# Cosine attention and a highway layer in one kernel: work shared out anew over the engines, and a new order

## The chip, the cores and the metric

The kernel runs on one core of one Trainium2 chip. The metric is device time in microseconds. A core has five instruction streams: PE (TensorE, products and transposes; its weight loads are shown as PEld), DVE (VectorE), ACT (ScalarE), POOL (GpSimd) and SP (SyncE, which here only issues transfers). Each works through its own instructions strictly in order and waits on semaphores for the others. ACT and POOL issue transfers too.

## The reference, cut to what matters

```python
# q, k, v: (8, 12, 448, 64) = batch, head, position, channel; float32
q_n = q / (norm(q, axis=-1) + 1e-06)
k_n = k / (norm(k, axis=-1) + 1e-06)
attn = softmax(q_n @ k_n.T / tau)            # tau = 0.1
x = (attn @ v) -> (8 * 448, 768)             # heads side by side
H = maximum(x @ w_h, 0)                      # w_h, w_t: (768, 768)
T = 1 / (1 + exp(-(x @ w_t + b_t)))
out = T * H + (1 - T) * x                    # float32
```

## The kernel before

**Tiling.** A batch has 12 heads, taken as three groups (g = 0, 1, 2) of four heads, two "t" by two "s". The 448 positions of a head are seven columns of 64 (NJ = 7). A tile of q or k holds 128 rows, 64 positions of two heads, and for a group 2 x 7 x 64 = 896 elements a row.

**Norms.** For each group of q and of k, `norm` squares the 896 elements (`sq`, line 359 on ACT; four k groups on POOL, line 362) and DVE sums each 64 of them (line 370, `rd2`). From the sums, 1/norm is made for several groups at once. Batch 0 uses a logarithm and an exponential on ACT (`lnexp`, lines 396 and 399). All others use `newton` (lines 381 to 388): a bit trick and two Newton rounds on DVE, seven instructions (`nt`), each of them an entry of its own in the order, so that other DVE work can stand between them. q's squares are scaled by tau, so that its 1/norm carries 1/tau.

**Scaling and turning.** `scale` (line 413) multiplies q and k by 1/norm on POOL into f16 (`qn`, 896 wide, and `kn`, in parts of 512 and 384). `turn` transposes them: early batches on PE (line 425, then a copy from PSUM on DVE, line 433), later ones by transposing transfers from SP (line 428).

**Attention.** PE makes scores (lines 468, 478; for batch 0 line 549), ACT takes their exponential (471, 481, 564), PE multiplies with the values (499, 507; 577, 597), and DVE divides by the row sums (514, 516; 579, 583) into `x`. Values are loaded by POOL in three transfers (lines 315 to 317) and copied into a tile with a column of ones (`vc`, DVE, line 439; the remaining 64 positions by `vt`, POOL, line 449).

**Highway layer.** A unit is 128 rows of `x`, four units a batch, 32 in all, the fourth of each batch half wide. `x` is transposed into `xT` (batch 0 on PE, later by a transfer from SP, line 628). PE multiplies with both weights (lines 659, 662). DVE adds the bias (`za`, 699), ACT takes a tanh (`th`, 713), DVE turns it into the gate 0.5 t + 0.5 (`gt`, 715), forms max(H, 0) - x (`hm`, 710) and multiplies by the gate (`gg`, 735). POOL adds x (`out`, 737), SP stores (744, 747). The last two units are split finer (677 to 732).

**What sets the order.** Nothing is scheduled when the kernel is built. `ORDER` at the top is a written-out list of all entries, 1498 of them; an engine's instructions run in the sequence in which they stand there. `SLOTS` says which buffer of a ring each tile takes, so the order also settles who must free a buffer for whom: the q tile `qr` has two buffers, so batch b's q load waits until POOL has scaled the q of batch b - 2. `HOLD` makes q loads wait for a named instruction. `PORT` names kinds of operation on DVE and POOL: the first such POOL instruction that follows a DVE one in the order waits for that DVE instruction.

**Loads.** q comes by SP as f32, k by POOL as f16 (batch 0's by SP and ACT as f32), the weights by POOL. In the list POOL's first entries are: identity, k of batch 1, the first scalings, three value loads of batch 0, `w_t`, the scalings of groups 1 and 2. `w_h`, k of batch 2 and the other values of batch 1 stand behind the scalings of batch 1's first group.

Of the kernel before, what the change touches and what calls it, by code (L numbers as in the profile page):

```python
# [10 lines left out]
I32 = mybir.dt.int32  # L11
# [9 lines left out]
1 4 24 25 2 6 26 0 242 21 17 27 14 19 29 3 16 18 12 28 9 22 13 5 8 11 40 15 20 42 7 10 43 36 38 41 37 39 52 53 44 68  # L21
65 64 239 45 71 66 46 70 69 32 67 72 256 47 31 50 30 73 54 33 51 114 55 48 88 90 74 112 115 49 246 257 78 75 56 252 77
247 57 248 241 85 240 79 76 91 80 84 113 249 98 96 81 89 86 258 259 60 87 99 260 63 61 82 97 59 58 62 122 261 253 254
92 93 120 94 262 123 95 83 116 121 101 263 117 264 100 280 250 118 138 429 119 106 255 35 276 125 139 124 107 126 102
130 127 103 131 279 104 251 136 128 105 277 245 281 278 129 34 108 109 282 137 430 110 146 111 144 265 175 147 244 266
140 176 141 243 145 132 267 133 268 152 434 134 142 269 179 135 270 177 143 442 192 180 153 193 149 271 178 443 294
438 148 194 286 181 23 196 154 150 283 309 151 195 155 435 197 310 305 198 287 156 306 157 307 158 611 439 160 308 288
275 284 161 159 184 433 285 209 436 289 293 186 210 162 444 290 301 163 299 437 185 302 187 164 300 445 165 440 610
220 166 221 188 182 333 297 967 441 167 334 218 274 219 168 298 446 169 431 273 170 303 447 432 222 171 211 212 304
448 183 213 272 199 449 172 450 321 173 325 451 322 174 214 200 452 317 215 461 326 313 323 316 457 324 312 295 291  # L30
625 315 292 327 460 619 331 296 318 314 311 626 332 201 464 203 328 319 202 320 462 617 475 329 463 345 330 474 458
189 204 459 346 357 190 205 342 338 358 349 335 206 350 347 468 353 618 340 337 348 336 226 467 341 354 227 339 490
343 355 613 344 491 465 789 469 356 466 351 362 455 470 360 352 359 456 620 361 621 615 480 366 363 454 365 481 364
478 367 486 471 368 479 228 229 487 616 385 482 484 483 233 453 234 230 401 485 472 235 476 623 473 492 369 493 477
973 488 504 622 388 489 788 386 624 387 799 505 389 627 231 495 499 628 216 506 629 502 614 390 496 503 494 790 497
630 498 631 370 507 232 612 236 371 217 207 391 500 510 501 508 511 372 373 392 509 632 237 393 374 395 795 633 538
800 512 650 514 539 396 394 515 377 397 638 513 379 516 223 797 528 536 974 519 523 640 529 639 517 518 796 378 537
647 380 417 635 530 641 381 526 531 520 521 644 238 522 527 409 524 398 411 793 525 532 224 534 966 410 535 651 794
642 412 533 643 542 645 399 540 801 798 666 668 541 667 546 413 544 652 545 669 547 543 418 653 548 803 549 660 656
977 419 661 804 550 404 375 402 802 646 403 657 191 405 971 637 664 406 662 566 814 423 663 1142 424 420 978 658 665  # L40
598 791 553 551 659 425 636 654 805 792 400 634 421 648 655 981 552 969 649 554 225 975 806 675 555 680 716 681 677
673 807 692 422 982 674 693 671 569 426 717 567 808 809 676 376 407 686 382 682 672 683 810 670 568 678 811 687 679
570 816 560 979 571 688 684 558 689 427 559 685 561 822 428 708 562 704 574 705 582 575 383 813 709 690 408 706 972
823 576 691 577 818 414 707 696 699 208 578 700 415 698 1156 714 976 710 817 701 572 604 819 697 980 599 715 830 600
711 605 983 984 601 968 820 556 606 694 824 695 821 1152 585 985 712 828 986 846 702 713 573 586 703 583 847 722 724
557 831 1141 987 1148 842 840 988 563 721 825 725 843 989 584 812 720 587 719 841 718 1317 723 602 838 726 834 1002
727 839 592 590 815 835 1153 728 844 564 836 845 593 579 826 829 837 591 994 827 832 588 594 870 760 853 871 852 833
850 996 858 1149 862 995 860 859 851 997 855 848 861 849 580 854 998 729 856 863 589 738 857 736 1150 1006 565 739
1157 1146 737 1007 744 868 740 1154 890 1001 731 732 1147 891 1004 730 1003 869 595 866 763 733 867 581 761 999 1151
864 894 888 865 764 1155 762 895 970 1000 873 878 765 889 876 877 1005 1021 1158 884 603 886 1022 879 875 874 885 776  # L50
872 747 880 991 887 745 607 993 881 748 1008 734 882 1144 892 1159 883 746 990 1145 384 752 749 893 1143 753 735 1009
608 1045 1160 1010 903 1161 899 1162 897 900 1046 992 898 902 596 896 1323 901 1015 904 1069 905 1016 754 755 1070 768
954 756 1017 1019 1018 1324 770 906 771 1020 769 741 766 922 1013 742 772 1037 777 1014 782 1163 1164 1316 1038 1011
1169 743 783 1012 1033 784 1035 778 416 767 1036 1176 1026 773 1030 1029 779 1034 1028 938 1027 1181 1039 1041 1061
# [792 lines left out]
```

## Time and profile before

| | |
|---|---|
| time, median of 3 runs | 282.19 us (281.32 to 286.61) |
| profiled execution | 279.05 us, its span 277.2 us |
| mean granted clock | 0.946 |
| HBM read, written | 39.12 MB, 11.01 MB |

The page of the profile gives the busy time of each engine as a share of the span, and the span in 40 slices of 6.93 us with the clock that PE was granted in tenths. The chain of work is followed back from the last instruction to what released it. A group's row reads: line, engine, operation, tiles, shapes, count, then busy us, mean ns of one, and idle time before it with what ended it. A waits row reads: who waited, for whom, total us, times, longest. Where an instruction row ends in square brackets, that is the engine's idle time just before it and what ended it.

### The profile page before, as it was taken

What the parts mean: (1) busy time and instruction counts of PE and PEld (TensorE: products, weight loads), DVE (VectorE), ACT (ScalarE), POOL (GpSimd) and SP (SyncE); (2) the same over time, 40 slices, a digit from 0 to 9 for tenths busy, and PEclk for the clock granted to TensorE, in tenths of its full rate; (3) what the DMA queues carried; (4) which work ended last, traced back from release to release, by engine and by line L of the source; (5) the groups of instructions that cost most, each with busy time, mean ns of one, the idle gap of its engine ahead of it and who ended that gap; (6) DMA issues with size and microseconds to landing.
All of it is one profiled execution on the core that took longest, in us unless ns stands there. A gap on an engine that the chain in (4) does not pass through costs nothing.

```text
span 277.2 us, 8206 instructions
## 1 busy us (share of the span) xinstructions
PE 238.2 (86%) x3447; PEld 146.5 (53%) x3447; DVE 213.9 (77%) x367; ACT 204.7 (74%) x253; POOL 169.5 (61%) x161
## 2 busy tenths in 40 slices
PE   8256799699989899498896999997999989999990
PEld 3135676365755565255554466564645755575640
DVE  3889669779999988639997678789776766446894
ACT  3396898799998989658788599996889568870230
POOL 2495829939837899138879645789348941330550
PEclk9856599999999999979999899999999999999998
DMA  7999599998599769996889979999879467238565
GB/s 229 290 176 254 161 246 204 216 275 104 60 162 263 115 177 223 135 197 120 125 228 166 201 136 175 194 272 196 113 177 163 82 147 162 66 75 194 139 154 144
DMA packets 77398, 47.93 MB, mean 173 GB/s; under 512 B 53040, under 2 KB 74160, under 8 KB 77360
## 3 DMA queue, kind: packets, MB, share of 16 engines
q1 hardware_dynamic: 54128, 33.57, 53.5%
q0 software_dynamic: 22800, 13.08, 35.1%
q10 hardware_dynamic: 432, 0.75, 0.8%
q8 instruction: 27, 0.44, 0.7%
q14 instruction: 11, 0.09, 0.1%
HBM read 39.12 MB, written 11.01 MB: 181 GB/s over the span
## 4 chain that ended last, share of the span: by engine, by line
PE 43%; DMA 21%; DVE 15%; POOL 10%; issue 6%; ACT 2%; DVEq 0%; POOLq 0%; ACTq 0%
PE banks L662 22%; DMA xT<-x 9%; PE banks L468 6%; PE banks L499 6%; DMA kr<-in_k_dram 6%; PE banks L659 4%; DMA qT<-qn 4%; POOL qn L413 3%; POOL kn L413 3%; DVE tt L715 2%; DVE hm L735 2%; DMA qr<-in_q_dram 2%; ACT E L471 2%; DVE x L516 2%; PE banks L478 1%
## 5 line engine op out<-in xcount | busy, mean ns | idle before, releaser
L471 ACT ACTIVATE E<-banks 128x896 f16<-128x896 f32 x126 | 109.7, 917 | 22.0 <-PE banks L468 20.0
L662 PEld LDWEIGHTS <-xT 128*128 128x128 f16 x576 | 51.9, 99 | 49.9 <-issue 14.1
L737 POOL TENSOR_TENSOR os<-x,hm 128x768 f32<-128x768 f16 (+1 forms) x30 | 44.7, 1493 | 42.9 <-DVE hm L735 20.2
L662 PE MATMUL banks<-wt,xT 128*128 128x384 f16 x288 | 55.3, 333 | 7.0 <-DMA xT<-x 6.9
L662 PE MATMUL banks<-wh,xT 128*128 128x384 f16 x288 | 55.6, 332 | 0.9 <-DVE hm L710 0.9
L370 DVE TENSOR_REDUCE n<-sq 128x14 f32<-128x896 f32 (+1 forms) x50 | 51.1, 1037 | 6.3 <-ACT sq L359 6.3
L413 POOL TENSOR_TENSOR qn<-qr,y 128x896 f16<-128x896 f32 (+1 forms) x24 | 41.0, 1710 | 23.2 <-issue 10.8
L413 POOL TENSOR_TENSOR kn<-kr,y 128x384 f16<-128x384 f16 (+1 forms) x42 | 40.0, 964 | 21.5 <-DVE y L388 7.8
L468 PE MATMUL banks<-qT,kT 64*64 64x448 f16 x504 | 40.0, 365 | 2.8 <-DVE x L516 1.7
L713 ACT ACTIVATE tt<-z 128x768 f16<-128x768 f32 (+1 forms) x32 | 24.2, 764 | 19.8 <-DVE z L699 19.2
L499 PE MATMUL banks<-vp,E 128*128 128x65 f16 x756 | 37.7, 194 | 0.0
L499 PEld LDWEIGHTS <-E 128*128 128x128 f16 x756 | 34.0, 97 | 6.5 <-issue 3.6
L710 DVE SCALAR_TENSOR_TENSOR hm<-banks,x 128x768 f16<-128x768 f32 (+1 forms) x30 | 25.7, 858 | 13.1 <-PE banks L662 10.2
L499 PE MATMUL banks<-vp,Et 128*128 128x65 f16 x252 | 34.3, 192 | 0.0
L699 DVE TENSOR_TENSOR z<-banks,bias 128x768 f32<-128x768 f32 x24 | 22.9, 952 | 9.6 <-PE banks L662 9.4
L359 ACT ACTIVATE sq<-qr 128x896 f32<-128x896 f32 (+1 forms) x24 | 22.1, 935 | 5.3 <-DMA qr<-in_q_dram 3.7
L499 PEld LDWEIGHTS <-Et 128*128 128x128 f16 x252 | 24.9, 99 | 0.0
L715 DVE TENSOR_SCALAR tt<-tt 128x768 f16<-128x768 f16 (+1 forms) x32 | 21.8, 683 | 2.7 <-ACT tt L713 2.7
L516 DVE TENSOR_TENSOR x<-banks,rd 128x896 f16<-128x896 f32 x21 | 22.9, 1089 | 0.5
L481 ACT ACTIVATE Et<-banks 128x896 f16<-128x896 f32 x21 | 19.0, 917 | 4.5 <-PE banks L478 4.4
L468 PEld LDWEIGHTS <-kT 64*64 64x64 f16 x504 | 12.6, 105 | 17.7 <-issue 15.2
L359 ACT ACTIVATE sq<-kr 128x896 f32<-128x896 f16 x17 | 16.1, 951 | 5.1 <-DMA kr<-in_k_dram 4.7
(74 smaller groups left out, 301.4 us busy)
## 6 DMA issues: line engine op xcount, KB each, us to landing
out_dram<-os SPq DMA_DIRECT2D x47, 192.0 KB, 3.3
qr<-in_q_dram SPq DMA_DIRECT2D x6, 1344.0 KB, 7.4
kr<-in_k_dram POOLq DMA_DIRECT2D x7, 672.0 KB, 12.9
vr<-in_v_dram POOLq DMA_DIRECT2D x8, 384.0 KB, 7.7
qr<-in_q_dram SPq DMA_DIRECT2D x6, 448.0 KB, 6.8
vr<-in_v_dram POOLq DMA_DIRECT2D x8, 288.0 KB, 9.4
out_dram<-os SPq DMA_DIRECT2D x15, 96.0 KB, 2.6
wt<-in_moe_w_t_dram POOLq DMA_DIRECT2D x1, 1152.0 KB, 13.8
```

The source lines that it names most:

```text
L359: nc.scalar.activation(dst, src, AF.Square, scale=sc)
L370: nc.vector.reduce_sum(R("n2", b)[:, c : c + 7 * n], a, axis=AX.X)
L413: ENG[eng].tensor_mul(o[:, :, t0:t1, :], a, y.unsqueeze(3).to_broadcast([128, hi - lo, t1 - t0, D]))
L468: nc.tensor.matmul(R("B", ("S", n, c))[64 * x : 64 * x + 64, t, 0:S], lhsT=keys(i, s, t, 2 * c + x), rhs=queries(t, s), start=True, stop=True)
L471: op("ACT", f"exp {n} {c}", lambda c=c, n=n: nc.scalar.activation(R("E", n)[:, 14 * c : 14 * c + 14, :].rearrange("l (t j) x -> l t (j x)" ...
L499: nc.tensor.matmul(U[:, 2 * c + t, :], lhsT=(E if m < NC else Et)[:, at : at + 2, :].rearrange("l j x -> l (j x)"), rhs=vp[:, 3 * t + m if ...
L516: op("DVE", f"ev14 {i}", lambda: nc.vector.tensor_mul(R("x", b)[:, :, 128 * g : 128 * g + 128].rearrange("l j (s d) -> l s j d", s=2), U_( ...
L662: nc.tensor.matmul(R("B", at)[:, mh, 0:MH], lhsT=xT[:, cc, :], rhs=w_[:, cc, MH * mh : MH * mh + MH], start=(cc == 0), stop=(cc == CC - 1))
L710: step("hm", n, lambda n=n, P=P: nc.vector.scalar_tensor_tensor(out=cut(R("hm", g), n), in0=P(n), scalar=0.0, in1=xs(n), op0=ALU.max, op1= ...
L713: op("ACT", f"th{nb} {g}", lambda: nc.scalar.activation(R("tt", g)[:, 0:W], R("z", g)[:, 0:W], AF.Tanh, scale=0.5), r=[("z", g), ("t0",)], ...
L715: op("DVE", f"gt{nb} {g}", lambda: nc.vector.tensor_scalar(out=R("tt", g)[:, 0:W], in0=R("tt", g)[:, 0:W], scalar1=0.5, scalar2=0.5, op0=A ...
L737: op("POOL", f"out{nb} {g}", lambda: nc.gpsimd.tensor_add(view(R("os", g)), xs(None), view(R("hm", g))), r=[("gg", g), xk], w=[("os", g)], ...
```

## The change

- `newton`: the seven steps are one entry of the order, and so stand together on their engine.
- tau leaves q's squares. The exponentials of the scores take `scale=1/tau` instead.
- `MOVED` names entries that run on another engine than their kind does. Gates (`gt`): 14 full and 3 half ones from DVE to POOL, among them the last unit's. Value copies (`vc`): seven full and two half ones from DVE to POOL. `vt`: eleven from POOL to DVE. Squares from ACT: with what was already elsewhere, 14 of 896 elements are now on POOL (four before) and nine of them and three halves on DVE (one half before). q loads: the first group of batch 1 and the whole of batches 4 to 7 are issued by ACT (five instructions).
- `FILL`: 46 products of zeros, of the kind of the 18 that the kernel begins with, into a PSUM buffer that nobody reads. 29 stand ahead of the first transpose, 8 ahead of the first scores, 4 and 5 around the second group's transposes.
- `PORT` loses the product with the gate (`gg`); `HOLD` keeps four entries of nine, for q loads that SP issues.
- A new order of all entries, and new buffers with it. POOL's first entries are now: identity, k of batch 1, the values of batch 0, both weights, k of batch 2, one value load of batch 1, then the first scaling. A square of batch 1 stands ahead of the third group's scaling. ACT takes the norms of group 1 ahead of the squares of batch 1. Batch 7's k load stands 32 entries ahead of the transposing transfer of unit 12 (14 before); batch 6's k load stands 14 entries behind that of unit 9 and 3 ahead of that of unit 10. The q loads of batches 4 to 7 on ACT stand 37, 34, 15 and 49 entries behind the scaling that frees their buffer.

```diff
-HOLD = {239: 44, 240: 57, 241: 252, 429: 121, 610: 56, 788: 57, 966: 53, 1141: 537, 1316: 161}
-
-PORT = ("nt", "gt", "gg", "vc", "qn", "kn", "vt", "out", "cx", "ou")
+HOLD = {240: 50, 241: 113, 417: 115, 592: 292}
+MOVED = {'sq1 q 0 0 0': 'DVE', 'vc3 0 3 0': 'POOL', 'vt 0 0': 'DVE', 'gt6 0': 'POOL', 'ldq 1 0': 'ACT',
...
+PORT = ("nt", "gt", "vc", "qn", "kn", "vt", "out", "cx", "ou")
...
-        o = Op(eng, name, fn, w, r, u, mode)
+        o = Op(MOVED.get(name, eng), name, fn, w, r, u, mode)
...
-    WARM, FILL, NLATE = 18, (), 2
+    WARM, FILL, NLATE = 18, (29, 8, 4, 5), 2
...
-                if eng == "ACT":
-                    nc.scalar.activation(dst, src, AF.Square, scale=sc)
-                elif eng == "POOL":
-                    assert sc == 1.0
-                    nc.gpsimd.tensor_mul(dst, src, src)
+                if on[-1] is nc.scalar:
+                    nc.scalar.activation(dst, src, AF.Square)
                 else:
-                    nc.vector.scalar_tensor_tensor(out=dst, in0=src, scalar=sc * sc, in1=src, op0=ALU.mult, op1=ALU.mult)
+                    on[-1].tensor_mul(dst, src, src)
...
-        def step(j):
+        def steps():
...
-            if j == 0:
-                v_.tensor_scalar(out=y.bitcast(I32), in0=n2.bitcast(I32), scalar1=-0.5,
-                                 scalar2=float(0x5F3759DF), op0=ALU.mult, op1=ALU.add)
-            elif j in (1, 4):
+            v_.tensor_scalar(out=y.bitcast(I32), in0=n2.bitcast(I32), scalar1=-0.5,
+                             scalar2=float(0x5F3759DF), op0=ALU.mult, op1=ALU.add)
+            for _ in range(2):
                 v_.tensor_mul(t, y, y)
...
-        for j in range(7):
-            op("DVE", f"nt{hi - lo} {b} {lo} {j}", lambda j=j: step(j), r=[("n2", b) + p for p in parts] if j == 0 else [("nt", i, j - 1)],
-               w=[("nt", i, j)] + ([("y", b) + p for p in parts] if j == 6 else []), u=[("tu", i), ("n2", b), ("y", b)])
+        op("DVE", f"nt{hi - lo} {b} {lo}", steps, r=[("n2", b) + p for p in parts], w=[("y", b) + p for p in parts],
+           u=[("tu", i), ("n2", b), ("y", b)])
...
-                op("DVE", f"gt{nb} {g}", lambda: nc.vector.tensor_scalar(
+                op("DVE", f"gt{nb} {g}", lambda: on[-1].tensor_scalar(
...
             for o in pl.ordered(ORDER, SLOTS):
                 n = len(nc.cur_bb.bb.instructions)
+                on.append(ENG[o.eng])
                 o.fn()
```

The loads, `scale`, `copy_v`, `copy_vt` and the output sum take their engine from `on[-1]` in the same way, and the exponentials get their scale; the lists `ORDER` and `SLOTS` are replaced.

75 lines of the change are left out of this document (36 added, 39 removed), and 110 rows, old and new, of the table ORDER.

## The prediction

> **What bounds the kernel now.** I read the page's busy times and slices first, then windows, then the chain of work that ended last.
>
> ```profile
> PE 238.2 (86%) x3447; PEld 146.5 (53%) x3447; DVE 213.9 (77%) x367; ACT 204.7 (74%) x253; POOL 169.5 (61%) x161
> PEclk9856599999999999979999899999999999999998
> PE 43%; DMA 21%; DVE 15%; POOL 10%; issue 6%; ACT 2%; DVEq 0%; POOLq 0%; ACTq 0%
> 0.00:20.00 20.00, 10.30 (x95) 5.58 (x95) 13.05 (x26) 10.58 (x18) 10.35 (x17) 0.79 1.03 231
> 20.00:40.00 20.00, 15.72 (x341) 13.00 (x342) 15.60 (x43) 16.69 (x22) 12.16 (x14) 0.70 0.88 221
> 60.00:80.00 20.00, 19.10 (x357) 13.15 (x355) 18.35 (x26) 19.58 (x25) 16.47 (x15) 1.00 0.86 118
> 76.70:200.40 123.70, 109.86 (x1529) 65.00 (x1524) 102.53 (x156) 101.49 (x125) 85.68 (x75) 0.97 1.01 178
> 220.00:240.00 20.00, 19.18 (x268) 11.50 (x266) 12.56 (x20) 13.42 (x18) 8.19 (x5) 1.00 0.69 145
> ```
>
> (A window's columns after its length: PE, PEld, DVE, ACT, POOL busy, each with its count; then clock, DMA share, GB/s.) No engine binds throughout. The first 40 us are a ramp: PE is busy 26.0 of 40, at clocks 0.79 and 0.70. From 60 to 80 us PE, DVE and ACT are all over 18 of 20, so taking work off one of them gives little. In the long middle none is above 89%, PE has 13.8 us of holes there, and POOL has most room (38 us). Late, only PE is full. DMA is a fifth of the chain. So a new order can win the ramp and the holes, not the full stages.
>
> **The ramp.** On the chain's pieces (start, length) and the waits:
>
> ```profile
> 13.24 0.71 POOL vr L317
> 13.95 0.75 POOL vr L316
> 14.70 0.75 POOL vr L315
> 15.44 0.84 POOL wt L321
> ...
> 16.75 1.70 POOL qn L413
> ...
> 34.07 16.36 DMA kr<-in_k_dram
> ```
> ```profile
> POOL qn L413 <- DVE kn L413: 8.4, 1, 8.4
> ```
>
> POOL's first four late loads (0.71 + 0.75 + 0.75 + 0.84 = 3.05 us) stand on the chain ahead of the second head group's scaling. The new order issues those four, both weights, batch 2's k and a third of batch 1's v ahead of the first scaling, in the 8.4 us in which POOL now only waits: 3.05 for the four and about 0.8 for each of three more, 5.5 us, fit. If that cover were gone, each would cost its 0.8 us. At most 3.05 is gained; next late are the second head group's norms, which ACT's new order takes before batch 1's squares. I take −2 (0 to −3.05). The k of batch 2, issued at 34.07 and landing 16.36 us later, leaves POOL some 25 us earlier; it held up ACT, and behind it PE:
>
> ```profile
> 50.51 0.95 ACT L359 ACTIVATE sq<-kr 128x896 f32<-128x896 f16 x1 [2.32 <-DMA kr<-in_k_dram]
> ```
>
> −2 (0 to −2.32); with DMA shares of 1.03 and 0.88 in the ramp the bytes cannot all come sooner, so not more.
>
> **The norm as one unit.** Seven Newton steps, now strung between other DVE work:
>
> ```profile
> 22.95 0.89 DVE L381 TENSOR_SCALAR y<-n 128x28 int32<-128x28 int32 x1
> ...
> 28.64 0.19 DVE L388 SCALAR_TENSOR_TENSOR y<-tu,y 128x28 f32<-128x28 f32 x1
> 29.06 0.84 POOL L413 TENSOR_TENSOR kn<-kr,y 128x384 f16<-128x384 f16 x1 [2.44 <-DVE y L388]
> ```
> ```profile
> POOL kn L413 <- DVE y L388: 7.8, 2, 5.3
> ```
>
> First to last is 5.88 us. At 0.89 for the first and six at about 0.19 they last 2.0 in a row, so the result can come 3.8 sooner; POOL waited 2.44 for it, on the chain, and 5.3 at a later norm, off it. −2 (0 to −2.44). The other side: DVE's queue behind the first step waits 2.0 us instead of pieces of it; that is at most 1 us for a PSUM read, seven times, mostly where DVE has room.
>
> **Products of zeros.** 46 matmuls of 512 columns. The clock is 0.5 to 0.6 in slices 3 to 5, 14 to 35 us, and transposes differ with it:
>
> ```profile
> 1.26 5.81 PE L280 MATMUL banks<-wz 128*128 128x512 f16 x18 [1.26 <-DVE wz L264]
> 12.19 0.93 PE L425 MATMUL banks<-ident,qn 128*128 128x128 f16 x7 [5.12 <-POOL qn L413]
> 46.58 0.56 PE L425 MATMUL banks<-ident,kn 128*128 128x128 f16 x7
> ```
>
> 18 take 5.81 us, 0.32 each, so the first 29 last at most 9.4 us, 5.6 at the ratio 0.56/0.93 of a fast clock, and end between 12.7 and 16.5, where the first transpose now starts at 12.19. The 17 behind (5.5 us at most) lie between transposes and products that wait anyway. Gain: 0.37 us for each of four early transposes, about −1.5; price: an overrun of 0.5 to 4.3 us. I take +0.5 (−1.5 to +4). The Trainium skill ("TensorE: Matmul & The Clock Gate", Part 1: The HAM clock gate) says the clock is halved by default, and opens after one busy window of about 3.4 us; by that the zeros keep it open if no gap is longer, and the term is its lower end (sum −11.5, time 275). The slices' 9, 8, 5 agree with a clock that falls when PE idles.
>
> **Work moved.**
>
> ```profile
> L715 DVE TENSOR_SCALAR tt<-tt 128x768 f16<-128x768 f16 x24 | 18.1, 759 | 2.1 <-ACT tt L713 2.1
> L715 DVE TENSOR_SCALAR tt<-tt x32: 242/354/2476, 57.7 to 270.9; 128x768 f16<-128x768 f16 x24, 128x384 f16<-128x384 f16 x8
> L439 DVE COPY vp<-vr 128x1152 f16<-128x1152 f16 x14 | 9.2, 657 | 0.0
> L449 POOL COPY vp<-vr 64x384 f16<-64x384 f16 x16 | 8.3, 520 | 7.9 <-DVE hm L735 4.6 <-issue 1.3 <-DMA vr<-in_v_dram 0.7
> masks.py:199 POOL TENSOR_SCALAR_AFFINE_SELECT ident<-ident 128x128 f16<-128x128 f16 x1 | 0.3, 292 | 0.1
> L362 POOL TENSOR_TENSOR sq<-kr 128x896 f32<-128x896 f16 x4 | 6.7, 1676 | 3.9 <-DVE n L370 3.8
> L359 ACT ACTIVATE sq<-qr 128x896 f32<-128x896 f32 x23 | 21.5, 951 | 5.3 <-DMA qr<-in_q_dram 3.7 <-DVE n L370 1.6
> L364 DVE SCALAR_TENSOR_TENSOR sq<-qr 128x448 f32<-128x448 f32 x1 | 0.6, 616 | 0.0
> ```
>
> Gates: 14 full and 3 half ones go to POOL. A gate's median on DVE is 0.354 and its worst 2.476: it waits there while POOL works. 14 × 0.759 = 10.6 us leave DVE. On POOL no gate is in the trace. Between a one-input 128-element operation (0.292) and a 384-element copy (0.520) the slope is 0.89 ns an element, which gives 0.86 for 768; the two-input 896-element square, 1.676, is the upper bound. I take 0.86, nearer in kind. The Trainium skill ("GPSIMD Engine Reference", 4.1 Engine selection) speaks against such moves: elementwise work belongs on VectorE, POOL being some twice as slow with two inputs and about line-rate with one. Squares agree (1.676 against ACT's 0.951). If line-rate means 768 elements at that page's 1.2 GHz, a gate would be an estimated 0.64 and POOL's sum 3 us less.
>
> Squares: POOL gains ten (16.8 us), DVE nine of 896 at up to 2 × 0.616 (11) and two halves; ACT loses 19 (18.1) and takes five q issues at 0.50:
>
> ```profile
> 0.74 0.50 ACTq L306 DMA_DIRECT2D E<-in_k_dram  x1
> ```
>
> Value casts: seven full go to POOL (by the slope 1.2 each, 8.4; upper 1.68), 4.6 us leave DVE; eleven 64-row casts (5.7) leave POOL for about 0.2 each on DVE. New sums: ACT 204.7 − 18.1 − 1.1 + 2.5 = 188; DVE 213.9 − 10.6 − 1.4 − 5.5 + 2.2 + 11 + 1.2 = 211; POOL 169.5 + 12.0 + 1.6 + 16.8 + 9.8 − 5.7 = 204. The longest engine stays PE. On the path: of DVE's share in the chain I credit the long gate waits, 17/32 of the four or five that stand there at 1.4 to 1.8: −2.5 (0 to −4). ACT's relief counts only in 60 to 80, where PE has 0.9 left: −0.5. POOL's square of batch 1 ahead of the third group's scaling puts +1.7 into the ramp, half of it covered: +1. The gate on POOL is 0.5 longer and queues; behind it wait only product, sum and store, no PSUM bank: 0, and up to 1 where it ends the tail.
>
> **Queues and holes.**
>
> ```profile
> PE banks L662 <- DMA xT<-x: 6.9, 4, 4.0
> 108.16 9.66 DMA xT<-x
> 143.12 8.46 DMA xT<-x
> SPq L300 <- POOL qn L413: 24.0, 3, 16.8
> ```
>
> Two transposes took 9.66 and 8.46 us, each issued beside a k load and v loads. The new order puts the last k load 32 places instead of 14 ahead of the transpose it met, but batch 6's k stays 3 ahead of one and 14 behind another. −2 (−5 to +3). The q loads of batches 1 and 4 to 7 leave SP, where three waited 24.0 us for POOL's scaling with transposes behind, for ACT. There a late one has the exponentials behind it, and PE behind those. By places (277.2 us / 1498 = 0.185 each) the plan leaves 6.8, 6.3, 2.8 and 9.1 us behind the scaling that frees the buffer, so I take 0 (to +12, rival below).
>
> Sum: −2 −2 −2 +0.5 −2.5 −0.5 +1 −2 = −9.5. When a wait goes the next late one takes part of it: I keep six tenths, −6, chosen because from 60 us three engines are nearly full. That is 273 where the profiled execution took 279.05 (span 277.2); the median of the runs, 282.19, is 3.1 above it, so I forecast **276**.
>
> **Rivals.** *All of it is kept*: the holes close too (−9.5, and 3.5 of the lower ends): 269. For it: PE is idle 39 us; against: the full stages. *Nothing arrives*: transfers set the ramp (shares about 1) and the same transposes meet loads; −1: 281. *POOL becomes the bound, and ACT waits for it*: in the middle row, 76.70 to 200.40 (end of batch 1's attention to end of batch 5's), POOL is busy 85.7 of 123.7. In the same stretch the new order, counted by names, adds seven squares (11.7), seven gates and a half one (6.5), three casts (3.6) and two q scalings (3.4), and takes out an output sum (1.7), three small casts (1.6) and a load: some 21, so 107, and 113 with gates at the upper bound. It decides once POOL's work and waits exceed some 118: scalings run late by more than the 3 to 9 us of slack, and q loads stop ACT, three times by about 4: +12 and −3 of the gains left, 291. For it: POOL waits in order for DVE, as rows above show; against: 11 to 17 us are still free. By that page of the Trainium skill a POOL twice as slow is what this rival needs; its one-input rate is what the forecast needs.
>
> **Chances.** Forecast 0.48 (own range 271 to 281), everything 0.16, nothing 0.17, POOL 0.19. The runs before spread from 281.32 to 286.61, so about 2% can be told from no change: 276.5 and 287.8. Some 0.27 of the forecast's 0.48 lies below 276.5: faster 0.27 + 0.16 = 0.43; within 2% 0.21 + 0.17 = 0.38; slower 0.19. The range 267 to 290 leaves out a quarter of the first rival and half of the last.
>
> **What would show it.** Right: k scaling without the 2.44 and 5.3 waits, squares of batch 2's k without a DMA wait, clock slices of 9 from 14 to 35 us, fewer gates above 1 us on DVE, POOL gates near 0.9. Wrong: exponentials that wait behind a q load on ACT, POOL above 90% between 77 and 200 us, transposes still at 8 to 10 us, PE waiting on DVE's scaled squares.

## The result: 3.7% slower, and the profile after

The changed kernel takes 291.50 us (291.24 to 291.81), the kernel before 281.75 in the same comparison; the ratio is 1.037 (1.031 to 1.043). I had forecast 276 and a range up to 290. Some executions of one kernel take one to three per cent longer than its others; ratios here compare the shorter ones, medians are of all. The page of the changed kernel, busy times and clock slices:

```profile
PE 247.5 (85%) x3493; PEld 149.7 (52%) x3493; DVE 235.7 (81%) x363; ACT 190.6 (66%) x232; POOL 206.6 (71%) x186
...
PEclk9997999979999798999999996999999999999996
```

ACT (190.6) and POOL (206.6) came out within 3 us of my 188 and 204. DVE did not: 235.7 where I had 211, and 213.9 before. PE is 9.3 us longer; the 64 products of zeros take 16.5 us, where the 18 before took 5.8. The second to fifth slice of the clock, 8, 5, 6 and 5 before, are now 9, 9, 7 and 9.

**Where the time went.** The prediction used one stage of the kernel before, from the last attention output of batch 1 to that of batch 5 (76.70 to 200.40, 123.70 us). Three pieces of it after, and then the whole of it (columns as in the prediction):

```profile
80.00:100.00 20.00, 16.38 (x181) 8.80 (x181) 18.70 (x29) 14.62 (x18) 15.89 (x14) 0.91 0.95 178
100.00:120.00 20.00, 17.36 (x261) 10.27 (x254) 18.60 (x22) 14.28 (x19) 15.42 (x14) 0.91 0.96 162
120.00:140.00 20.00, 16.52 (x224) 9.73 (x222) 18.96 (x27) 13.70 (x17) 16.18 (x15) 1.00 1.24 160
...
79.74:212.59 132.85, 112.79 (x1528) 66.41 (x1524) 118.37 (x163) 93.48 (x113) 106.06 (x90) 0.95 0.94 160
```

The profiled span grew by 12.8 us, from 277.2 to 290.0: 3.0 of it ahead of the stage (79.74 against 76.70), 9.15 in it, 0.6 behind. In the stage, length minus PE's busy time gives PE's holes: 13.8 before (123.70 − 109.86), 20.1 after. So 6.2 of the 9.15 are new holes, and 2.9 are PE's own work, which took longer at a granted clock of 0.95 instead of 0.97. In the three pieces DVE is busy 18.6 to 19.0 of 20 us; ACT and POOL have more room. From 140 to 200 us it is less, 17.2, 17.8 and 14.5 of 20, and PE's holes there are nearly as large (9.2 us in 60, against 9.7 in the three pieces), so DVE does not fill every part of the stage. These two readings, holes and clock, are used for every run below.

Which instructions of DVE grew? One row of the kernel before that the prediction lacks, the product of gate and hidden row:

```profile
L735 DVE TENSOR_TENSOR hm<-tt,hm 128x768 f16<-128x768 f16 x23 | 14.7, 644 | 0.2
```

and the groups of the kernel after (count, busy us, mean ns):

```profile
L726 DVE TENSOR_TENSOR hm<-tt,hm 128x768 f16<-128x768 f16 x23 | 23.6, 1032 | 1.5 <-POOL tt L707 1.4
...
L441 DVE COPY vp<-vr 64x384 f16<-64x384 f16 x11 | 8.5, 771 | 0.2
L360 DVE TENSOR_TENSOR sq<-qr 128x896 f32<-128x896 f32 x4 | 7.7, 1920 | 1.3 <-DMA qr<-in_q_dram 1.3
L360 DVE TENSOR_TENSOR sq<-kr 128x896 f32<-128x896 f16 x5 | 7.1, 1428 | 0.0
L707 DVE TENSOR_SCALAR tt<-tt 128x768 f16<-128x768 f16 x10 | 6.9, 693 | 1.6 <-ACT tt L705 1.6
...
L360 POOL TENSOR_TENSOR sq<-kr 128x896 f32<-128x896 f16 x7 | 12.2, 1756 | 0.3 <-DVE tt L707 0.3
...
L707 POOL TENSOR_SCALAR tt<-tt 128x768 f16<-128x768 f16 x14 | 12.9, 923 | 17.8 <-ACT tt L705 10.2 <-DVE y L381 4.9 <-DVE vp L441 1.6
```

Against my terms: the product +8.9 (I had nothing for it), the eleven 64-row casts 8.5 (2.2), the nine squares 14.8 (11). The gate on POOL is 0.92 (0.86). The timelines of DVE and of POOL show what the extra time is (start, length):

```profile
129.38 2.60 DVE L360 TENSOR_TENSOR sq<-qr 128x896 f32<-128x896 f32 x1
...
137.19 1.60 DVE L360 TENSOR_TENSOR sq<-kr 128x896 f32<-128x896 f16 x1
```
```profile
129.00 2.02 POOL L405 TENSOR_TENSOR qn<-qr,y 128x896 f16<-128x896 f32 x1
...
136.12 1.72 POOL L405 TENSOR_TENSOR qn<-qr,y 128x896 f16<-128x896 f32 x1
```

POOL's two scalings end at 131.02 and 137.84; DVE's squares, begun while they ran, end 0.96 and 0.95 us later. Each stood still until POOL was done, then worked for about a microsecond. In the page's sums a stalled instruction counts as busy, the first of these squares with its whole 2.60. Last, the waits, one of the kernel before and three of the kernel after:

```profile
ACT E L471 <- PE banks L468: 20.0, 25, 5.5
```
```profile
ACT E L463 <- PE banks L460: 41.0, 42, 3.7
...
PE banks L460 <- DVE z L691: 5.5, 6, 3.1
...
ACT sq L358 <- DMA kr<-in_k_dram: 0.6, 1, 0.6
```

ACT waits for scores 41.0 us, 20.0 before; PE in turn waits for DVE, above all for it to read PSUM banks. Among the eleven longest groups of PE's waits, those for DVE (but the one for the zeros at the start) sum to 19.3 us after and to 3.8 before. The wait of a square for batch 2's k, 2.32 before, is gone, as forecast; the 0.6 in the last row is an earlier one.

### The profile page after: what moved, and what is told of

Same layout as the page of the kernel before. It is cut to its first block, busy times and chain, and to the rows that moved or that the text cites. A ratio compares the mean times of both kernels' runs of the same rounds, so it can differ in the third digit from the quotient of the medians.

```text
span 290.0 us, 8307 instructions
## 1 busy us (share of the span) xinstructions
PE 247.5 (85%) x3493; PEld 149.7 (52%) x3493; DVE 235.7 (81%) x363; ACT 190.6 (66%) x232; POOL 206.6 (71%) x186
## 4 chain that ended last, share of the span: by engine, by line
PE 22%; DVE 16%; POOL 6%; issue 4%; DMA 3%; ACT 1%; DVEq 0%; POOLq 0%; ACTq 0%
PE banks L654 11%; PE banks L491 4%; PE banks L460 3%; DMA xT<-x 3%; DVE n L366 2%; DVE z L691 2%; DVE hm L702 2%; POOL kn L405 2%; DVE hm L726 2%; POOL os L728 2%; DVE vp L441 1%; PE banks L651 1%; DVE tt L707 1%; DVE x L508 1%; POOL qn L405 1%
## 5 line engine op out<-in xcount | busy, mean ns | idle before, releaser
L654 PE MATMUL banks<-wh,xT 128*128 128x384 f16 x288 | 57.4, 340 | 6.4 <-DVE hm L702 3.3
L728 POOL TENSOR_TENSOR os<-hm,x 128x768 f32<-128x768 f16 (+1 forms) x30 | 44.2, 1477 | 18.8 <-DVE hm L726 6.9
L405 POOL TENSOR_TENSOR kn<-kr,y 128x384 f16<-128x384 f16 (+1 forms) x42 | 41.4, 993 | 21.4 <-DVE rd L571 5.9
L654 PE MATMUL banks<-wt,xT 128*128 128x384 f16 x288 | 53.3, 327 | 2.1 <-DMA xT<-x 1.8
L460 PE MATMUL banks<-qT,kT 64*64 64x448 f16 x504 | 41.3, 378 | 11.4 <-DVE z L691 5.5
L491 PE MATMUL banks<-vp,E 128*128 128x65 f16 x756 | 38.6, 196 | 2.1 <-DVE z L691 1.1
L491 PEld LDWEIGHTS <-E 128*128 128x128 f16 x756 | 35.0, 99 | 9.4 <-issue 7.0
L726 DVE TENSOR_TENSOR hm<-tt,hm 128x768 f16<-128x768 f16 (+1 forms) x30 | 28.6, 961 | 2.0 <-POOL tt L707 1.9
L707 POOL TENSOR_SCALAR tt<-tt 128x768 f16<-128x768 f16 (+1 forms) x17 | 14.4, 850 | 21.4 <-ACT tt L705 11.0
L556 ACT ACTIVATE E<-banks 128x768 f16<-128x768 f32 (+2 forms) x21 | 18.0, 922 | 6.1 <-PE banks L541 4.5
```

Source lines behind the costliest of these rows:

```text
L405: on[-1].tensor_mul(o[:, :, t0:t1, :], a, y.unsqueeze(3).to_broadcast([128, hi - lo, t1 - t0, D]))
L460: nc.tensor.matmul(R("B", ("S", n, c))[64 * x : 64 * x + 64, t, 0:S], lhsT=keys(i, s, t, 2 * c + x), rhs=queries(t, s), start=True, stop=True)
L491: nc.tensor.matmul(U[:, 2 * c + t, :], lhsT=(E if m < NC else Et)[:, at : at + 2, :].rearrange("l j x -> l (j x)"), rhs=vp[:, 3 * t + m if ...
L654: nc.tensor.matmul(R("B", at)[:, mh, 0:MH], lhsT=xT[:, cc, :], rhs=w_[:, cc, MH * mh : MH * mh + MH], start=(cc == 0), stop=(cc == CC - 1))
L726: op("DVE", f"gg{nb} {g}", lambda: nc.vector.tensor_mul(R("hm", g)[:, 0:W], R("tt", g)[:, 0:W], R("hm", g)[:, 0:W]), r=[("gt", g), ("hm", ...
L728: op("POOL", f"out{nb} {g}", lambda: on[-1].tensor_add(view(R("os", g)), view(R("hm", g)), xs(None)), r=[("gg", g), xk], w=[("os", g)], u= ...
```

## The experiments

Two theories stood at first. **P, the port**: DVE's fast and two-input instructions stand still while POOL works; work was added on both sides, DVE became the longest engine in batches 2 to 5, and that is the loss. **O, the order**: the new order itself loses. All runs below but the first change either the kernel after ("new order") or the kernel before ("old order"). The diffs are cut; where a line picks entries of `MOVED` by a rule, the kernel that ran has the entries so picked written out.

### What one instruction pays

A kernel of single instructions, which computes nothing of the reference: DVE goes through eight kinds in turn, with POOL idle, with POOL multiplying, and with POOL doing gates.

> A kernel of its own that computes nothing of the reference: the DVE instructions in question (896-element f32 square, 768-element f16 product, 768-element f16 gate, 64-row and 128-row f16 copies, 896-element sum, and two reads of PSUM with one SBUF operand), first with POOL idle, then while POOL runs 896-element products without a pause, then while POOL runs 768-element gates. Theory P: with POOL busy the square goes from 1.0 to 1.5-2.7 us, the product from 0.48 to 1.0-2.0, gate and copies from 0.25-0.45 to 1.0-2.0, while the sum (1.07) and the PSUM reads (0.95) stay. If it were memory traffic in general, all would stretch by a like share; if the instructions are only slow in the kernel for another reason (their operands, transfers), nothing changes beside POOL. A gate on POOL takes 0.8-0.9 us alone.

Groups of DVE with POOL idle:

```profile
L37 DVE TENSOR_TENSOR sq<-a 128x896 f32<-128x896 f32 x8 | 8.6, 1071 | 0.0
L41 DVE TENSOR_REDUCE n<-a 128x14 f32<-128x896 f32 x8 | 8.5, 1067 | 0.0
L43 DVE TENSOR_TENSOR z<-bank,a 128x768 f32<-128x768 f32 x8 | 7.5, 939 | 0.0
...
L38 DVE TENSOR_TENSOR hm<-a,b 128x768 f16<-128x768 f16 x8 | 4.3, 541 | 0.0
...
L39 DVE TENSOR_SCALAR tt<-a 128x768 f16<-128x768 f16 x8 | 2.7, 343 | 0.0
L40 DVE COPY vp<-a 64x384 f16<-64x384 f16 x8 | 1.9, 242 | 0.0
```

and beside POOL's products of 896 elements:

```profile
L51 POOL TENSOR_TENSOR pn<-p,y 128x896 f16<-128x896 f32 x28 | 63.3, 2260 | 2.2
L38 DVE TENSOR_TENSOR hm<-a,b 128x768 f16<-128x768 f16 x6 | 14.5, 2420 | 0.0
L39 DVE TENSOR_SCALAR tt<-a 128x768 f16<-128x768 f16 x6 | 13.3, 2220 | 0.0
L40 DVE COPY vp<-a 64x384 f16<-64x384 f16 x6 | 12.8, 2127 | 0.0
...
L41 DVE TENSOR_REDUCE n<-a 128x14 f32<-128x896 f32 x6 | 6.4, 1069 | 0.0
L37 DVE TENSOR_TENSOR sq<-a 128x896 f32<-128x896 f32 x5 | 6.1, 1225 | 0.0
L43 DVE TENSOR_TENSOR z<-bank,a 128x768 f32<-128x768 f32 x5 | 4.7, 944 | 0.0
```

and two of them beside POOL's gates:

```profile
L40 DVE COPY vp<-a 64x384 f16<-64x384 f16 x6 | 5.3, 880 | 0.0
L38 DVE TENSOR_TENSOR hm<-a,b 128x768 f16<-128x768 f16 x5 | 2.7, 542 | 0.0
```

Beside POOL's products the short ones pay most: product 0.54 to 2.42, gate 0.34 to 2.22, 64-row cast 0.24 to 2.13, each 1.9 more, about one POOL product. Sums and reads of PSUM pay nothing. The square paid 0.15 at its place in this sequence, less than I had expected; in the kernel it took 0.4 to 0.8 more than alone here. POOL loses a little: 2.26 a product, and 2.07 once DVE has stopped (146 to 161 us). Beside POOL's gates it is the other way round. From 165 us on only the 64-row cast of DVE's kinds pays, 0.24 to 0.88, while a gate on POOL takes 1.22 us beside DVE (165 to 198 us) and 0.83 alone (203 to 245 us). Which engine pays thus depends on what meets what. The Trainium skill ("SBUF — State Buffer", Who interferes with whom) states this as a lock: a copy or one-input operation of DVE in a two-port mode excludes POOL, two SBUF inputs exclude a POOL instruction that reads SBUF, and whoever comes second waits for the whole of the other; reductions never contend. The rows beside POOL's products agree, in the square only by its 0.15; beside its gates POOL waits more than DVE does, which that rule allows. The prediction weighed the page on POOL and not this one.

### One part undone at a time

```diff
-PORT = ("nt", "gt", "vc", "qn", "kn", "vt", "out", "cx", "ou")
+PORT = ("nt", "gt", "gg", "vc", "qn", "kn", "vt", "out", "cx", "ou")
```

> The changed kernel with the product with the gate (gg) put back among the kinds that a later POOL instruction waits for; nothing else differs. Theory P (port): DVE instructions that read two SBUF operands, or copy at the fast rate, stand still while a POOL instruction runs, and the 22 us more of DVE time cost the 10 us. Then the product's mean falls from 1032 to about 650 ns, DVE from 235.7 to some 226, and the time from 291.5 to 286-289; if POOL's waits cost as much as they save, the time stays. Theory O (order): what lost the time is who stands behind whom in the new order, and DVE's longer instructions fill time that was idle anyway: DVE falls, the time stays at 291 +-1.

288.12 us, ratio 1.024 (1.020 to 1.028). Its groups of DVE and its row for the stage:

```profile
L726 DVE TENSOR_TENSOR hm<-tt,hm 128x768 f16<-128x768 f16 x23 | 18.1, 790 | 1.6 <-POOL tt L707 1.4
...
L360 DVE TENSOR_TENSOR sq<-qr 128x896 f32<-128x896 f32 x4 | 8.1, 2030 | 1.2 <-DMA qr<-in_q_dram 1.2
L360 DVE TENSOR_TENSOR sq<-kr 128x896 f32<-128x896 f16 x5 | 8.0, 1613 | 0.0
```
```profile
79.90:207.58 127.68, 108.24 (x1519) 65.16 (x1516) 116.18 (x164) 92.23 (x112) 102.41 (x89) 0.99 0.97 165
```

The guard (a later POOL instruction waits for the product) takes 5.5 us off the product, yet DVE's whole sum falls only by 1.3 (234.4): the squares, the other casts and the half products now stall instead. The holes hardly change, 19.4. What got shorter is PE's own work, 112.8 to 108.2, at a clock of 0.99. The same edit the other way round, in the old order:

> The kernel before with the product with the gate taken out of the kinds that a later POOL instruction waits for. Theory P: the product's mean rises from 644 to 800-1000 ns, DVE from 213.9 to 218-222, POOL runs on earlier; the time is between no change and +2%. Theory O: 282 +-1, since the order is that of before.

280.42 us, ratio 0.995 (0.990 to 0.999), DVE 214.7. The product rose to 0.736, less than theory P expected. Alone in the old order, dropping the guard costs nothing. In the new order putting it back won 3.4 us, a time that theory P had forecast, but by the clock and not by the holes; so what the guard is worth where DVE is full stays open.

```diff
-... 'sq2 k 1 2 0': 'DVE', 'sq2 q 2 1 0': 'DVE', 'sq2 k 3 1 0': 'DVE', 'sq2 k 3 2 0': 'DVE', 'sq2 q 5 2 0': 'DVE',
-... 'sq2 q 6 0 0': 'DVE', 'sq2 k 6 2 0': 'DVE', 'sq2 q 7 1 0': 'DVE', 'sq2 k 7 1 0': 'DVE',
```

> The changed kernel with the nine full squares of DVE back on ACT, at the same places of the order. Theory P: DVE loses their 14.8 us (235.7 to about 221) and ACT gains 8.6 (190.6 to 199); the time falls by 5 to 9, to 283-287. Theory O: ACT's exponentials stand behind nine more squares, DVE only idles more: 290-293.

284.97 us, 1.013 (1.009 to 1.017), DVE 221.4: the largest of the three parts, −6.5. In the stage:

```profile
77.08:206.10 129.02, 113.28 (x1526) 67.01 (x1523) 111.26 (x159) 96.49 (x118) 105.72 (x90) 0.95 0.97 164
```

Holes fall to 15.7, and the stage begins at 77.1 instead of 79.7; the clock stays at 0.95.

```diff
-... 'vt 0 0': 'DVE', 'vt 0 1': 'DVE', 'vt 1 1': 'DVE', 'vt 3 0': 'DVE', 'vt 4 0': 'DVE', 'vt 4 1': 'DVE',
-... 'vt 5 0': 'DVE', 'vt 5 1': 'DVE', 'vt 6 0': 'DVE', 'vt 6 1': 'DVE', 'vt 7 1': 'DVE',
```

> The changed kernel with the eleven 64-row value copies of DVE back on POOL. Theory P: DVE loses 8.5 us, POOL gains 5.7; the time falls by 1 to 4, to 287.5-290.5. A POOL-bound theory (POOL late, others wait for it) expects +1 to +4. Theory O: 291 +-1.

291.45 us, 1.035 (1.032 to 1.039). Theory P as I had put it, with 8.5 us of casts to win, missed here: DVE's sum fell by 2.4, to 233.3, while gates (0.69 to 0.94) and the other groups grew. A stall that is taken away from one instruction is found by the next.

### The order with and without its moved work

All three undone together, and then nothing moved at all:

```diff
+MOVED = {n: e for n, e in MOVED.items() if not n.startswith("vt") and not (n.startswith("sq2") and e == "DVE")}
...
-PORT = ("nt", "gt", "vc", "qn", "kn", "vt", "out", "cx", "ou")
+PORT = ("nt", "gt", "gg", "vc", "qn", "kn", "vt", "out", "cx", "ou")
```

> The changed kernel with three parts undone together: the product of gate and hidden row guarded again, the nine full squares back from DVE to ACT, the eleven 64-row value casts back on POOL. Theory P (the shared port: DVE's two-input products and copies wait for POOL, and DVE's sum sets the time): DVE's busy time falls to 214 to 218 us, and the time to 281 us (279 to 284). Theory O (the new order itself loses): no better than with the squares alone put back, 285 us or more, though DVE's sum is as before.

280.99 us, 1.001 (0.997 to 1.005).

```diff
-MOVED = {'sq1 q 0 0 0': 'DVE', 'sq1 k 0 0 1': 'DVE', 'vc3 0 3 0': 'POOL', 'vc3 0 3 1': 'POOL', ...
+MOVED = {}
...
-PORT = ("nt", "gt", "vc", "qn", "kn", "vt", "out", "cx", "ou")
+PORT = ("nt", "gt", "gg", "vc", "qn", "kn", "vt", "out", "cx", "ou")
```

> The changed kernel's order with none of its work moved to another engine: gates, squares, casts and q loads are all where they were before, the product is guarded again. What is left of the change is the new order, the Newton unit and the products of zeros. Theory P: DVE near 214 us, ACT near 206, POOL near 170, and 280 us (277 to 284), since only the moved work costs. Theory O: 286 us or more.

279.96 us, 0.994 (0.989 to 0.999). (The four k squares that POOL has in the kernel before are on ACT here.) Theory O, that the new order by itself loses, is out: order, Newton unit and zeros together cost nothing and win at most 1%. The stage, first without moved work, then of the run above:

```profile
77.48:200.03 122.55, 111.01 (x1539) 65.53 (x1540) 102.71 (x164) 103.51 (x128) 80.58 (x74) 0.97 0.98 173
```
```profile
77.87:200.71 122.84, 109.14 (x1519) 65.24 (x1516) 106.59 (x154) 95.47 (x116) 105.05 (x94) 0.97 0.96 171
```

All squares back on ACT, everything else moved (the diff drops the 25 entries that begin with `sq`):

> The changed kernel with every moved square back on ACT, those of POOL too; all else as changed. With DVE's nine alone put back it took 285 us. If DVE is slow because POOL's two-input squares hold it up, DVE falls under the 221 us of that run by 5 or more, POOL to 188, ACT rises to 207, and the time is 281 us (278 to 283). If DVE's own work alone counts, 285 (283 to 287). If ACT's relief was worth something, the time rises over 287.

281.91 us, 1.003 (0.998 to 1.008), DVE 214.7, POOL 180.8: 3 us less than with only DVE's nine put back. Last, the zeros:

```diff
-    WARM, FILL, NLATE = 18, (29, 8, 4, 5), 2
+    WARM, FILL, NLATE = 18, (1, 1, 1, 1), 2
```

> The changed kernel with one product of zeros in each of the four groups instead of 29, 8, 4 and 5. PE's busy time falls by some 8 us. Theory P: the ramp's transposes run at a lower clock again in 14 to 40 us, and because DVE sets the stages behind, the time stays at 291 us (289 to 294). If the zeros were what costs the order its time, 288 us or less.

289.88 us, 1.036 (1.031 to 1.040). PE's busy time falls by 4.8 us, not by the 8 expected. Its clock slices:

```profile
PEclk9757599999999988997997998899999999999997
```

The early clock falls again to 7, 5, 7 and 5, and the end of batch 1 comes at 80.00 us, against 79.74 with the zeros. They do what they are for, keep the clock up, and the time does not gain by it. That the clock stands low without them agrees with what the prediction cited of the Trainium skill ("TensorE: Matmul & The Clock Gate", Part 1: The HAM clock gate); its term's lower end, a gain, did not come.

### Parts of the change in the old order

```diff
-258 259 60 87 99 260 63 61 82 97 59 58 62 122 261 253 254
+258 259 260 261 262 263 264 60 87 99 63 61 82 97 59 58 62 122 253 254
```

Entries 258 to 264 of the order are the seven steps of the first unit; the other seven units likewise.

> The kernel before, in whose order the seven Newton steps of each norm stand together at the place of the first step; nothing else differs. My prediction's term for it: 2 us faster (0 to 2.44), so 279.7 where the kernel before takes 281.7. Rival: the results come sooner but nothing that sets the end waits for them, so 281 to 283.

281.45 us, 0.996 (0.992 to 1.001): some 1 us less, and anything from 2.4 less to no gain fits. So neither my −2 nor the rival is excluded. The wait itself went: POOL's k scalings waited 7.8 us for the norms' last step before and 1.2 here. But POOL's idle time ahead of them, whatever ended it, is 21.5 us before and 23.3 here: other waits took its place.

```diff
-    SQV = ()
+    SQV = (("k", 1, 2), ("q", 2, 1), ("k", 3, 1), ("k", 3, 2), ("q", 5, 2), ("q", 6, 0), ("k", 6, 2), ("q", 7, 1), ("k", 7, 1))
```

> The kernel before with nine full squares on DVE instead of ACT (the nine that the change moves there, but k of batch 3, second group, from POOL), in the old order and with all guards of before. Theory P (work put on DVE beside POOL costs the time, in whatever order): DVE's busy time rises by 10 to 17 us to 224 to 231, and the time by 3 to 6 us to 285 to 288. Theory O (only the new order makes them harmful): 281 to 283.

284.76 us, with single times from 278.71 to 288.48, too scattered for a ratio. DVE rose to 224.5, the low end of the expectation. (These squares are another two-input instruction than the changed kernel's, line 364.) Whether DVE's squares cost as much in the old order stays open.

### The squares taken apart

In the new order with nothing else moved (the product guarded, and `MOVED` cut to the nine full squares on DVE, the fourteen on POOL, or both):

```diff
+MOVED = {n: e for n, e in MOVED.items() if n.startswith("sq2") and e == "DVE"}
...
+MOVED = {n: e for n, e in MOVED.items() if n.startswith("sq2") and e == "POOL"}
...
+MOVED = {n: e for n, e in MOVED.items() if n.startswith("sq2")}
```

> The changed order with nothing moved but the nine full squares on DVE (product guarded). Without them this order took 280 us with DVE busy 213. Theory P1 (their work on DVE costs by itself): DVE 224 to 230 and 284 to 287 us. Theory P2 (they cost only together with the squares on POOL): DVE 222 to 225, 280 to 282 us.

> The changed order with nothing moved but the fourteen full squares on POOL (product guarded). P1: POOL 187, ACT 195, and the time as without them or less, 278 to 281 us, since DVE keeps its 213 and ACT is relieved. P2: DVE's other work waits for POOL, DVE rises to 218 or more, 282 to 284 us.

> The changed order with all squares moved as the change has them, nine to DVE and fourteen to POOL, and no gate, cast or q load moved (product guarded). P1: the time of the nine alone, within 1 us. P2: 3 us or more above either part alone, 286 to 289 us, with the mean of a square on DVE near 1.6.

On DVE: 280.91 us, 0.999 (0.994 to 1.004). On POOL: 276.86 us, 0.983 (0.980 to 0.985). Both: 284.16 us, 1.009 (1.006 to 1.011). Against 279.96 with none moved, that is +1, −3 and +4; two independent parts would have given −2. P1 is out by the first run; P2 has the time of the first right and is 5 and 2 us too high in the others. The stage of the three, in the same order:

```profile
78.05:199.97 121.92, 108.98 (x1539) 65.19 (x1536) 109.89 (x169) 100.26 (x124) 80.88 (x74) 0.99 1.00 174
```
```profile
77.88:196.61 118.73, 106.43 (x1523) 64.18 (x1520) 107.75 (x164) 95.33 (x116) 95.83 (x83) 1.00 1.01 177
```
```profile
79.90:204.53 124.63, 107.94 (x1519) 65.02 (x1516) 114.74 (x170) 91.72 (x112) 96.79 (x83) 0.99 0.99 169
```

DVE's time adds up: 102.7 with none, +7.2 by its own squares, +5.0 by POOL's, +12.0 with both. The holes don't: 11.5, 12.9, 12.3, 16.7. DVE at 103 to 110 in a stage of 120 costs PE nothing; at 115 it does. This is the step that does not add up. Nor do the two parts slow each other much: a square on DVE is hardly slower beside POOL's squares (1.76 and 1.40 us by kind) than without them (1.75 and 1.29).

### Gates, casts and q loads

Squares on POOL as above, and with them the gates (first line), or the casts and q loads (second):

```diff
+MOVED = {n: e for n, e in MOVED.items() if n.startswith("sq2") and e == "POOL" or n.startswith("gt")}
...
+MOVED = {n: e for n, e in MOVED.items() if n.startswith("sq2") and e == "POOL" or n.startswith(("vc", "ldq"))}
```

> The changed order with the fourteen squares on POOL (277 us alone) and the seventeen gates on POOL too, product guarded, casts and q loads not moved. With the seven casts and five q loads moved as well it took 281. Theory G (POOL's load is what costs: 186 + 13 = 200 us, and what waits for it): 280 to 281 us. Theory D (taking work off DVE still pays): DVE falls from 220 to 212 or less, and the time to 275 to 277.

281.10 us, 1.001 (0.997 to 1.004): +4.2 on the squares alone. Its row of the stage and the gates that stay on DVE:

```profile
77.56:201.12 123.56, 109.84 (x1523) 65.81 (x1520) 107.49 (x156) 95.04 (x116) 101.74 (x91) 0.97 0.98 169
```
```profile
L707 DVE TENSOR_SCALAR tt<-tt 128x768 f16<-128x768 f16 x10 | 11.0, 1099 | 1.9 <-ACT tt L705 1.9
```

> The changed order with the fourteen squares on POOL, the seven full casts and two halves of batch 0 on POOL, and the five q loads issued by ACT; gates not moved, product guarded. Theory G: POOL 186 + 10 = 196, 279 to 280 us. If casts and q loads cost nothing and the gates made the 4 us between 277 and 281: 276 to 278.

276.49 us, 0.986 (0.979 to 0.993): casts and q loads cost nothing. Its stage:

```profile
77.13:195.83 118.70, 106.03 (x1520) 63.96 (x1520) 107.73 (x161) 95.07 (x116) 98.94 (x86) 1.00 1.05 176
```

So theory G's load of POOL hardly decides it (195.0 here, 199.5 with the gates). Gates gone from DVE left its stage at 107.5, as without: the ten full ones that stay take 1.10 us each, where all 24 took 0.67. Of the 4.8 us that the stage grew, 3.4 are PE's work at 0.97 instead of 1.00, and 1.4 are holes; why the clock is lower stays open.

The clock shows in the last pair too, gates alone with one zero in each group, and the same with four k squares on POOL:

```diff
+MOVED = {n: e for n, e in MOVED.items() if n.startswith("gt")}
...
+MOVED.update({f"sq2 k {b} 1 0": "POOL" for b in range(2, 6)})
```

> The changed kernel's order, with only the gates left on POOL, the product guarded again, squares, casts and q loads as in the run that moved nothing, and one product of zeros in each group. That run took 280 us with DVE busy 213 us. Theory P: the gates leave DVE (10 us less by their old mean of 0.76) and cost POOL 14, which has room: DVE 203 to 207, POOL 177, and 277 to 280 us. If DVE is no longer what sets the time once the squares are gone: 279 to 281, the same. If POOL's gates hold DVE up as the squares did: over 281.

> The run with only the gates moved and one product of zeros in each group (278 us, DVE 210, ACT 208, POOL 176), and four squares of k on POOL instead of ACT, as the kernel before has them. If ACT's 208 us set the stages from 40 to 185: ACT 204, POOL 183, 276 to 278 us. If a square on POOL costs DVE more than it gives ACT: 278 to 280. Either way it should stay below the kernel before by 1% or more.

278.14 us, 0.988 (0.980 to 0.996), and 284.28 us, 1.010 (1.006 to 1.014). The stage of each:

```profile
77.63:197.87 120.24, 107.94 (x1539) 64.24 (x1540) 102.12 (x157) 103.59 (x128) 86.84 (x82) 1.00 1.07 176
```
```profile
78.64:204.42 125.78, 112.22 (x1539) 67.17 (x1536) 103.26 (x156) 102.55 (x126) 89.99 (x84) 0.96 0.98 168
```

With the gates alone DVE's sum fell by 2.4 (212.6 to 210.2), not by the 10 expected: its other gates grew from 0.57 to 0.80. No expectation covers 284. Of the 5.5 us between the two stages 4.3 are PE's same work at 0.96 instead of 1.00, and 1.3 holes. What lets the clock fall is not settled, and the two rows are of unlike executions: 277.01, the shortest of its kernel, and 285.76, the second longest of six.

### All runs on two readings

| run | time, us | stage | PE's holes | DVE busy | clock |
|---|---|---|---|---|---|
| before | 281.8 | 123.7 | 13.8 | 102.5 | 0.97 |
| before, norm as one unit | 281.5 | 124.5 | 15.8 | 100.8 | 0.97 |
| before, product unguarded | 280.4 | 126.6 | 16.2 | 103.8 | 0.96 |
| before, squares on DVE | 284.8 | 129.4 | 18.9 | 108.9 | 0.97 |
| nothing moved | 280.0 | 122.6 | 11.5 | 102.7 | 0.97 |
| gates, few zeros | 278.1 | 120.2 | 12.3 | 102.1 | 1.00 |
| the same, 4 squares on POOL | 284.3 | 125.8 | 13.6 | 103.3 | 0.96 |
| after, three parts undone | 281.0 | 122.8 | 13.7 | 106.6 | 0.97 |
| after, all squares on ACT | 281.9 | 125.4 | 13.2 | 107.3 | 0.97 |
| squares and gates on POOL | 281.1 | 123.6 | 13.7 | 107.5 | 0.97 |
| squares on POOL, casts, q loads | 276.5 | 118.7 | 12.7 | 107.7 | 1.00 |
| squares on POOL | 276.9 | 118.7 | 12.3 | 107.8 | 1.00 |
| squares on DVE | 280.9 | 121.9 | 12.9 | 109.9 | 0.99 |
| after, DVE's squares on ACT | 285.0 | 129.0 | 15.7 | 111.3 | 0.95 |
| squares on both | 284.2 | 124.6 | 16.7 | 114.7 | 0.99 |
| after, guarded | 288.1 | 127.7 | 19.4 | 116.2 | 0.99 |
| after, 64-row casts on POOL | 291.5 | 131.6 | 19.9 | 116.7 | 0.96 |
| after, few zeros | 289.9 | 132.5 | 19.7 | 116.8 | 0.95 |
| after | 291.5 | 132.9 | 20.1 | 118.4 | 0.95 |

In the new order (from "nothing moved" on) the holes stand at 11.5 to 13.7 while DVE is busy up to 110 us in the stage, and rise from there to 20 at 118. That is theory P's part, and for the new order it is shown. In the old order the holes are larger at the same time on DVE, 13.8 to 16.2 at 101 to 104 us and 18.9 at 109, so DVE's time is not all that makes them. The clock comes on top, without a plain relation to DVE. Stage, holes and clock are of one profiled execution, the time is a median, and some of these kernels scatter: the one with nothing moved ran from 276.64 to 282.73, and its row is of an execution of 280.86, the second longest of ten. So the clock of a row may belong to the execution as much as to the kernel; the holes rest on firmer ground.

## Why the prediction was wrong

**The step that failed** is the sum "DVE 213.9 − 10.6 − 1.4 − 5.5 + 2.2 + 11 + 1.2 = 211. ... The longest engine stays PE". It measured 235.7. I took every price on DVE as a property of the instruction, and so the eleven casts "for about 0.2 each": that is right alone (0.242), and was 0.771 here. I had the sign of it before me, "it waits there while POOL works", but applied it only to the gates that leave, not to what stays and comes while POOL's work rises by 37 us. The product's lost guard got no term at all. Of the 24.7 us that the sum missed, the product with its halves is 11.1, the casts are 6.3 and the squares 3.8. The second half of the sentence failed with it: in batches 2 to 5 DVE, at 118.4 of 132.9 us, is longer than PE.

**Squares.** "nine of 896 at up to 2 × 0.616 (11)" were 14.8, a small miss in size. What weighed was where they went: together with POOL's squares they bring DVE to the height at which PE's holes grow, +7.3 us over POOL's squares alone.

**Gates off DVE, −2.5.** Not found: DVE's stage stayed at 107.5, the time rose by 4.2 beside POOL's squares, most of it by the clock. Without those squares the gates moved (and few zeros) gave 278.1 against 280.0, inside the scatter of the latter. The price on POOL, 0.86, was right: 0.92 in the kernel, 0.83 alone. The Trainium skill's page on POOL ("GPSIMD Engine Reference", 4.1 Engine selection), which I had weighed as speaking against the move, leans the right way here: 0.92 on POOL, where DVE alone needs 0.34, and the 0.64 worked out from its line rate is further off than 0.86. The prediction's "Squares agree" set POOL's 1.676 against ACT's 0.951; the page speaks of DVE, which alone takes 1.071.

**The ramp: −2, −2, −2 and +0.5.** The steps are seen, the gain isn't. The DMA wait for batch 2's k is gone, four of the first five slices are at 9, and yet batch 1 ends at 77.5 us with nothing moved and at 76.7 before. Newton as a unit, alone in the old order, gave some −1 (0 to −2.4). In the window from 0 to 66.5 us, here before and with nothing moved, the bytes flow alike:

```profile
0.00:66.50 66.50, 50.16 (x853) 33.97 (x854) 50.41 (x112) 50.97 (x66) 42.16 (x50) 0.85 1.08 224
```
```profile
0.00:66.50 66.50, 54.25 (x880) 33.91 (x881) 50.94 (x109) 50.56 (x64) 38.70 (x48) 0.95 1.10 225
```

With DMA shares of 1.08 and 1.10 and 224 and 225 GB/s, my rival's reason, transfers that set the ramp, fits; no run tried it. The 3.0 us that the changed kernel loses ahead of the stage come with DVE's squares beside POOL's: the stage begins at 77.1 to 78.6 without DVE's, at 78.1 with DVE's alone, and at 79.7 to 80.1 in the runs that have both.

**ACT's relief, −0.5, was too small.** With POOL's squares alone ACT falls to 198.5 us, and the time to 276.9, my forecast; against the profiled execution with nothing moved (its second longest), though, the stage gains 3.8 us, made of 4.6 less of PE's work at a better clock and 0.8 more of holes. So the number agrees by a way that I had not argued.

**The rivals.** *POOL becomes the bound, and ACT waits for it* gave 291, the time that came, by a mechanism that did not. POOL in the stage was 106.1, my 107, below the 118 from which it was to decide, and 80% busy; ACT issued its q loads without waiting, and with the casts moved to POOL and the q loads to ACT the time was 276.5. With the three parts undone POOL is busy 208.5 us, more than in the changed kernel (206.6), and the time is 281. The engine that filled up was the one beside it. POOL's work still counts: on the chain that ended last of the kernel after, DVE alone stands from 142.6 to 152.9 us, but almost only POOL from there to 174.4. *Nothing arrives* describes the order alone (280). *All of it is kept* is nowhere; the best run is 276.5.

**Queues and holes, −2.** Not separated by a run. The holes of the order with nothing moved are 2.3 us smaller than before, which is as much. PE's waits for transposes of x fell from 6.9 us to 1.8 in the kernel after.

## What to carry to other kernels

Where two engines hold each other up, price an operation by what the other will be doing then: beside POOL's two-input products, short two-input operations, gates and casts on DVE cost four to nine times their own length, and an undone stall moved to the next such instruction rather than vanish. Sum an engine over the stage that decides, with the new work on both sides. In this order nothing was lost while DVE was busy for up to some nine tenths of the stage (109.9 of 121.9 us); of the 8.5 us more that it has in the changed kernel, PE's holes show 7.1. Split a stage's time into PE's holes and PE's busy time before giving a few microseconds to a cause, since the granted clock can make or hide that much.

## What I had not expected

- A product on DVE beside a POOL busy with products took 2.42 us instead of 0.54; POOL's own took 2.26 instead of 2.07. Beside POOL's gates the product kept its 0.54, and the gates took 1.22 instead of 0.83.
- Putting eleven casts back, 8.5 us by their group, changed DVE's sum by 2.4 and the time by nothing.
- The same work of PE in the stage took from 106.0 us at a clock of 1.00 (squares, casts and q loads moved) to 113.3 at 0.95 (all but DVE's squares moved).
- The version with only POOL's squares moved (276.86, 0.983) and that with the casts and q loads as well (276.49, 0.986) beat both kernels, by less than 2% over the kernel before.
